# An attention, MoE and MoE kernel: thresholds and reciprocal sums placed behind later scores' bias, the bias as a one-operand multiplication, zero products in the first unit

## The chip, the cores and the metric

The kernel runs on one core of one Trainium2 chip. The metric is the device time of one execution in microseconds (us). An execution before the change takes 652.03 us in the median of three runs (651.8 to 654.82). The engines are TensorE (PE in the profile, with its weight loads as PEld), VectorE (DVE), ScalarE (ACT), GpSimd (POOL) and SyncE (SP), each with its own queue that runs in order.

## The reference

Three layers in a row. The first is an attention over 2 batches of 8 heads, 768 positions and 64 channels, in which a query sees a key only if the signs of six random projections agree:

```python
q_bits = (np.einsum('bhsd,dk->bhsk', q, proj) > 0).astype(np.int64)
k_bits = (np.einsum('bhsd,dk->bhsk', k, proj) > 0).astype(np.int64)
mask = q_bucket[:, :, :, None] == k_bucket[:, :, None, :]
scores = scale * np.matmul(q, k.transpose(0, 1, 3, 2))
scores = np.where(mask, scores, -1000000000.0)
scores = scores - np.max(scores, axis=-1, keepdims=True)
attn = np.exp(scores)
attn = attn / (np.sum(attn, axis=-1, keepdims=True) + 1e-09)
return np.matmul(attn, v).astype(np.float32)
```

Its result, as 1536 rows of 512, goes through a mixture of 8 experts with a fixed capacity (`x @ w_gate`, greedy assignment, two matrices per expert), and then through a second mixture with a skip gate and the best expert per row. The change touches the attention alone.

## The kernel before

Attention is cut into 16 units: a pair of heads and half of the queries (384). A unit has six score tiles of 128 queries by 768 keys, three per head. The mask is computed inside the score product: beside the 64 channels the key and query tiles carry 12 rows that hold thresholded projections, so that a pair with different signs gets a score that is lower by a large power of two. A head's keys are kept as K1 (a rounded copy) and K2 (the rest, and in rows 64 to 76 the thresholds); Q1 and Q2 are the same for queries.

For each tile, `score(u, i)` issues two products with Q1 and K1 (L197) and two with Q2 and K2 (L199) into one of two S buffers, and on the DVE a reduction over 768 keys (L201), the gate g (L202) and the bias b (L203). `expo` runs the exponential on ACT (L210), which reads S, b and g and frees the S buffer. Transposes (L219), their copies on ACT (L222) and the value products (L233) follow some tiles later. At tile 5 of the value products the sums get their reciprocal (L239, L240), which `fin` needs one unit later for the scaling of the rows it transposes back (L276 to L278).

While a unit runs, the next ones are prepared: `loadq` and `loadk` issue the DMAs on SP, `splitq` and `splitk` make Q1, Q2, K1 and K2 (a copy on DVE or, in unit 0, ACT; a subtraction on POOL, L139 and L152), and `project` multiplies queries and keys with the signs on PE (L168) into a small PSUM tile named aux, of which there is one copy. The thresholds (L174 for Q, L182 for K) read it on the DVE. `project` is a generator that stops once: the first two thresholds are issued at once, the others at the next odd tile (`left`). The tile of `fin` and the product tile of the routing counts (`count0`, L597) are taken from the same single buffer, tag aux.

Nothing is scheduled by a planner in this stage: the loop over units u and tiles i at the end of `attention` writes each engine's queue in the order of the calls. The tables `splits`, `projs` and `setup` say what is called at (u, i); `kplan` says which heads' keys are split in a unit: one head in units 0 to 4 and 9, two in units 5 to 8, none later. The second one of a unit is split and projected at tile 5. `awake` (L40) issues products of zeros whose result nobody reads; before the change there are 20 of them at the program's start.

## Time and profile before

| | |
|---|---|
| median of the runs | 652.03 us |
| the profiled execution | 652.32 us |
| its span, first to last instruction | 650.5 us |
| mean granted TensorE clock | 0.965 |
| PE busy | 597.1 us, 92% of the span |
| DVE busy | 494.0 us, 76% |
| ACT busy | 399.9 us, 61% |
| POOL busy | 162.9 us, 25% |
| reductions L201, 96 | 91.6 us, 18.7 idle before them |
| exponentials L210, 96 and their sums' reads | 95.1 us, 39.5 idle before them, 34.6 of it for the bias |

Attention fills the span's first 277 us or so, the two mixtures the rest. Shares of busy time are averages over these stages. A product counts as busy from its issue to its modelled end, and products overlap. The granted clock is given as a share of 2.4 GHz, and has two levels here, 1.0 and 0.5 (1.2 GHz). In a timeline row the bracket at its end gives how long the engine had been idle before it and who ended that.

### The profile page before, as it was taken

How to read it: one execution, taken by the hardware profiler on the slowest of the kernel's cores; microseconds unless marked ns; L12 is line 12 of the kernel's file. 1: busy time of each engine (PE TensorE's matmuls, PEld its weight loads, DVE VectorE, ACT ScalarE, POOL GpSimd, SP SyncE). 2: the span in 40 equal slices, each digit the busy share in tenths (PEclk: the TensorE clock that was granted, in tenths of full speed). 3: DMA queues.
4: the chain of work that ended last, by engine and by line, in shares of the span. 5: the costliest groups of instructions: out<-in, count | busy, mean ns of one | idle time of the engine just before them, and what ended most of it. 6: DMA issues, size and time to landing. Idle time of an engine off the chain costs nothing.

```text
span 650.5 us, 11417 instructions
## 1 busy us (share of the span) xinstructions
PE 597.1 (92%) x3781; PEld 434.6 (67%) x3781; DVE 494.0 (76%) x1542; ACT 399.9 (61%) x909; POOL 162.9 (25%) x212
## 2 busy tenths in 40 slices
PE   7889989999999999866878899999999999999994
PEld 3666666666666667745647487686786778777873
DVE  6888889999888786574958776877633467999991
ACT  4767767777677777412425654554554556887881
POOL 2245234334121120241013131221502322311110
PEclk8789999999999999957989999999999999999998
DMA  6114223312301010054367837458665379999800
GB/s 222 59 61 112 98 73 116 104 51 74 91 21 38 1 49 3 2 193 143 130 200 264 281 75 260 168 175 270 214 226 170 112 287 351 387 384 318 312 10 26
DMA packets 53240, 99.69 MB, mean 153 GB/s; under 512 B 6422, under 2 KB 12950, under 8 KB 53169
## 3 DMA queue, kind: packets, MB, share of 16 engines
q1 hardware_dynamic: 42016, 76.21, 34.9%
q10 hardware_dynamic: 7072, 13.63, 5.8%
q0 software_dynamic: 4080, 8.99, 4.2%
q8 instruction: 34, 0.56, 0.4%
q14 instruction: 38, 0.30, 0.2%
HBM read 88.72 MB, written 12.46 MB: 156 GB/s over the span
## 4 chain that ended last, share of the span: by engine, by line
PE 30%; DVE 10%; issue 6%; DMA 4%; ACT 2%; POOL 1%; POOLq 0%; DVEq 0%; ACTq 0%
PE ph L1173 10%; PE y L1198 6%; DVE wlo L1360 5%; PE y L1204 4%; DMA out<-o,ixi 3%; PE pr L1242 1%; DMA xg<-xd,idsb 1%; PE py L1422 1%; PE py L1421 1%; PE py L1420 1%; PE pxt L1152 1%; PE ph L1420 1%; ACT whi L1359 1%; PE ph L1421 1%; PE ph L1422 1%
## 5 line engine op out<-in xcount | busy, mean ns | idle before, releaser
L1360 DVE TENSOR_TENSOR wlo<-w,whi 128x512 fp32r<-128x512 f32 x192 | 123.7, 686 | 24.9 <-ACT whi L1359 20.9
L210 ACT ACTIVATE P<-S,b,g 128x768 f32<-128x768 f32 x96 | 95.1, 991 | 39.5 <-DVE b L203 34.6
L1359 ACT ACTIVATE whi<-w 128x512 fp32r<-128x512 f32 x192 | 109.4, 622 | 0.4 <-issue 0.4
L1173 PE MATMUL ph<-xT,w 128*128 128x192 f32 x512 | 103.3, 346 | 4.6 <-PEq L1526 4.6
L201 DVE TENSOR_REDUCE nm<-S 128x1 f32<-128x768 f32 x96 | 91.6, 954 | 18.7 <-PE S L199 17.1
L1173 PEld LDWEIGHTS ph<-xT,w 128*128 128x128 f32 x512 | 84.3, 195 | 13.9 <-issue 8.4
L222 ACT ACTIVATE PT<-pT 128x512 f32<-128x512 f32 x135 | 75.8, 593 | 25.6 <-PE pT L219 24.5
L219 PE MATMUL pT<-idf,P 128*128 128x128 f32 x576 | 81.3, 277 | 0.5 <-ACT PT L225 0.3
L219 PEld LDWEIGHTS pT<-idf,P 128*128 128x128 f32 x576 | 68.1, 143 | 5.7 <-ACT mrow L576 0.8
L197 PE MATMUL S<-K,Q 128*128 128x512 f32 x192 | 60.1, 395 | 12.8 <-ACT P L210 12.2
L233 PE MATMUL av<-PT,vd 128*64 128x384 f32 x360 | 67.8, 498 | 0.0
L197 PEld LDWEIGHTS S<-K,Q 128*128 128x128 f32 x192 | 30.1, 197 | 44.3 <-issue 21.4
L152 POOL TENSOR_TENSOR Q<-qd,Q 64x384 fp32r<-64x384 f32 x30 | 36.2, 1208 | 79.4 <-PE av L233 28.5
L1178 ACT ACTIVATE h<-ph 128x128 f32<-128x128 f32 x64 | 17.7, 276 | 60.5 <-PE ph L1173 29.5
L199 PE MATMUL S<-K,Q 76*128 76x512 f32 x192 | 51.0, 348 | 1.8 <-DVE Q L174 1.8
L233 PEld LDWEIGHTS av<-PT,vd 128*64 128x64 f32 x360 | 22.0, 136 | 23.8 <-issue 23.8
L199 PEld LDWEIGHTS S<-K,Q 76*128 76x128 f32 x192 | 30.6, 195 | 6.4 <-issue 2.1
L139 POOL TENSOR_TENSOR K<-kd,K 64x768 fp32r<-64x768 f32 x15 | 27.2, 1814 | 27.3 <-DVE K L130 18.8
L1204 PE MATMUL y<-w,h 128*64 128x512 f32 x128 | 32.3, 610 | 0.0
L1321 POOL DMA_INDIRECT tb<-rec,ii x16 | 16.0, 999 | 64.7 <-DVE cnt L1318 48.4
L1422 PE MATMUL py<-whi,hl 128*128 128x512 f32 x72 | 29.3, 406 | 1.4 <-DVE hl L1431 1.4
L1462 POOL DMA_INDIRECT out<-o,ixi x9 | 10.5, 1169 | 79.1 <-DVE o L1454 47.1
(374 smaller groups left out, 1125.1 us busy)
## 6 DMA issues: line engine op xcount, KB each, us to landing
w<-w SPq DMA_DIRECT2D x28, 1024.0 KB
w<-u SPq DMA_DIRECT2D x26, 1024.0 KB
kd<-kT SPq DMA_DIRECT2D x16, 384.0 KB
qd<-qT SPq DMA_DIRECT2D x32, 192.0 KB
w<-u ACTq DMA_DIRECT2D x6, 1024.0 KB
w<-w ACTq DMA_DIRECT2D x4, 1024.0 KB
xd<-X SPq DMA_DIRECT2D x4, 780.0 KB
vd<-v SPq DMA_DIRECT2D x16, 192.0 KB
```

What stands on the lines that cost most here:

```text
L197: nc.tensor.matmul(S[:, n0:n1], d["Q1", a][:, ts], kd["K1"][:, n0:n1], start=True, stop=False)
L199: nc.tensor.matmul(S[:, n0:n1], d["Q2", a][:, ts], kd["K2"][:, n0:n1], start=False, stop=True)
L201: nc.vector.tensor_reduce(d["nm"][:, c], S, op=ALU.max, axis=AX.X, negate=True)
L210: nc.scalar.activation(P, S, AF.Exp, bias=d["b"][:, c], scale=d["g"][:, c], accum_out=d["s"][:, c])
L219: nc.tensor.transpose(p[:, a, b, :], d["P"][2 * ip + b][:, (2 * cp + a) * 128:(2 * cp + a + 1) * 128], self.idf)
L222: nc.scalar.activation(dst, p.rearrange("p a b q -> p a (b q)"), AF.Copy)
L233: nc.tensor.matmul(d["av"][64 * a:64 * a + 64, :], VH[b * 8 + 2 * p + a][:, c, :], d["PT"][:, c, a * 384:(a + 1) * 384], start=(c == 0), s ...
L1173: nc.tensor.matmul(ph, w1[f // 4][:, d, f % 4 * 128:f % 4 * 128 + 128], xT[:, d, :], start=(d == 0), stop=(d == 3))
L1204: nc.tensor.matmul(y2[64 * h:64 * h + 64, :], h2[:, 4 * h + f, :], res["w2"][h][:, f, :], start=(f == 0), stop=(f == 3))
L1359: nc.scalar.activation(hi[:, c, :], w[:, c, :], AF.Copy)
L1360: nc.vector.tensor_tensor(lo[:, c, :], w[:, c, :], hi[:, c, :].bitcast(F32), op=ALU.subtract)
L1422: nc.tensor.matmul(out, a[1][:, i, :], hi[:, i % 4, :], start=False, stop=stop)
```

## The change

Four edits, all in `attention`.

`project` no longer issues thresholds. It issues the products and returns the generators, and the loop puts each threshold either at once or into a table `due`, under the number of a later score tile; `score` takes what is due for its tile and issues it behind the tile's bias. Of the four thresholds of a unit's projection at tile 1, the first stays there, the second goes behind the bias of tile 2, the K pair behind that of tile 4. Of a projection at tile 5 (units 5 to 8), one K threshold stays, the second goes behind the bias of the next unit's tile 0. At the program's start the second Q threshold goes behind the bias of tile 0, and the K pair of head 1 behind that of tile 1. Sums and reciprocal, now in `sums`, go behind the bias of tile 4, one tile later than before.

The bias b is computed by `tensor_scalar` with the gate as a per-partition scalar, where it was a `tensor_tensor` of two tiles.

In unit 0, 20 products of zeros stand between the first tile's two kinds of score products, and 5 behind each of tiles 1, 2 and 3. They write the transposes' PSUM tile.

In unit 0, the splits are issued behind the exponential of their tile, and that of head 2 moves from tile 1 to tile 2. `keys` makes K1 and K2 for whichever comes first, the split or a threshold.

```diff
             def project(fs, tag="aux"):
                 gs = [f(x, y, p[32 * i:32 * i + 12], i) for i, (f, x, y) in enumerate(fs)]
                 for g in gs:
                     next(g)
-                for i, g in enumerate(gs):
-                    next(g)
-                    if i == 1:
-                        yield
+                return gs
...
+                g0 = u * 6 + i
...
+                if g0 == 0:
+                    busy(20)
                 for n0, n1 in ((0, 512), (512, 768)):
                     nc.tensor.matmul(S[:, n0:n1], d["Q2", a][:, ts], kd["K2"][:, n0:n1], start=False, stop=True)
...
-                nc.vector.tensor_tensor(d["b"][:, c], d["g"][:, c], d["nm"][:, c], op=ALU.mult)
+                nc.vector.tensor_scalar(d["b"][:, c], d["nm"][:, c], d["g"][:, c], None, op0=ALU.mult)
+                for f in due.pop(g0, []):
+                    f()
+                if 0 < g0 < 4:
+                    busy(5)
+
+            def busy(k):
+                self.awake(ps.tile([128, 2, 2, 128], F32, name="pT", bufs=2).rearrange("p a b q -> p (a b q)")[:, 0:256], k)
...
-                    r = d["r"] = sm.tile([128, 6], F32, name="r")
-                    nc.vector.tensor_scalar(r, d["s"], 1e-9, None, op0=ALU.add)
-                    nc.vector.reciprocal(r, r)
+            def sums(u):
+                r = UD[u]["r"] = sm.tile([128, 6], F32, name="r")
+                nc.vector.tensor_scalar(r, UD[u]["s"], 1e-9, None, op0=ALU.add)
+                nc.vector.reciprocal(r, r)
...
-            for _ in project([(projk, 0, 0), (projk, 0, 1), (projq, 0, 0), (projq, 0, 1)]):
-                pass
+            due = {}
+            x = project([(projk, 0, 0), (projk, 0, 1), (projq, 0, 0), (projq, 0, 1)])
+            for f in x[:3]:
+                next(f)
+            due[0] = [lambda f=x[3]: next(f)]
...
+            for u in range(2, NU):
+                due.setdefault(u * 6 + 4, []).append(lambda u=u: sums(u - 2))
...
-                    for f, *x in splits.get((u, i), []):
-                        f(*x, ceng=nc.scalar if u == 0 else nc.vector)
+                    for f, *x in splits.get((u, i), []) if u else []:
+                        f(*x)
...
                     expo(u, i)
+                    for f, *x in [] if u else splits.get((u, i), []):
+                        f(*x, ceng=nc.scalar)
...
                         if (u, i) in projs:
-                            left = project(projs[u, i])
-                            next(left, None)
+                            fs = project(projs[u, i])
+
+                            at = (g + 1, g + 1, g + 1, g + 1) if u == 0 and i == 0 else (g, g + 1, g + 3, g + 3)
+                            for f, x in zip(fs, at):
+                                if x == g:
+                                    next(f)
+                                else:
+                                    due.setdefault(x, []).append(lambda f=f: next(f))
```

On the DVE at the program's start, the first two score tiles (nm, g and b are reduction, gate and bias; K2 and Q2 with a number are the threshold rows of head 0, of the first two query tiles, and of head 1). Before:

```order
L182 TENSOR_SCALAR K2_144<-aux_163,thr_77 12x384 x2
L174 TENSOR_SCALAR Q2_150<-aux_163,thr_77 12x384
L174 TENSOR_SCALAR Q2_159<-aux_163,thr_77 12x384
L201 TENSOR_REDUCE nm_184<-S_188 128x1
L202 TENSOR_SCALAR g_185<-nm_184 128x1
L203 TENSOR_TENSOR b_186<-g_185,nm_184 128x1
L182 TENSOR_SCALAR K2_173<-aux_198,thr_77 12x384 x2
L201 TENSOR_REDUCE nm_184<-S_203 128x1
```

The same place now:

```order
L185 TENSOR_SCALAR K2_144<-aux_163,thr_77 12x384 x2
L177 TENSOR_SCALAR Q2_150<-aux_163,thr_77 12x384
L207 TENSOR_REDUCE nm_183<-S_187 128x1
L208 TENSOR_SCALAR g_184<-nm_183 128x1
L209 TENSOR_SCALAR b_185<-nm_183,g_184 128x1
L177 TENSOR_SCALAR Q2_159<-aux_163,thr_77 12x384
L207 TENSOR_REDUCE nm_183<-S_222 128x1
L208 TENSOR_SCALAR g_184<-nm_183 128x1
L209 TENSOR_SCALAR b_185<-nm_183,g_184 128x1
L185 TENSOR_SCALAR K2_172<-aux_219,thr_77 12x384 x2
```

The second Q threshold, the last reader of the first aux tile, has moved behind the first bias, and the K pair of head 1, the last reader of the second aux tile, behind the second bias.

On PE at the same place, from the end of the first score tile to the second's end; aux_219 is the projection of head 1's keys, in the buffer that aux_163 had. Before:

```order
L199 MATMUL S_188<-K2_144,Q2_150 128x256
L168 MATMUL aux_198<-kd_141,prs_135 12x384 x2
L197 MATMUL S_203<-K1_143,Q1_149 128x512
L197 MATMUL S_203<-K1_143,Q1_149 128x256
L199 MATMUL S_203<-K2_144,Q2_150 128x512
L199 MATMUL S_203<-K2_144,Q2_150 128x256
L168 MATMUL aux_230<-qd_180,prs_135 12x384
```

The same place now, with the last of the 20 zero products ahead and the first of five behind:

```order
L40 MATMUL pT_190<-zero_71 128x256
L205 MATMUL S_187<-K2_144,Q2_150 128x512
L205 MATMUL S_187<-K2_144,Q2_150 128x256
L171 MATMUL aux_219<-kd_141,prs_135 12x384 x2
L201 MATMUL S_222<-K1_143,Q1_149 128x512
L201 MATMUL S_222<-K1_143,Q1_149 128x256
L205 MATMUL S_222<-K2_144,Q2_150 128x512
L205 MATMUL S_222<-K2_144,Q2_150 128x256
L40 LDWEIGHTS zero_71
L40 MATMUL pT_232<-zero_71 128x256
```

PE's projection still stands ahead of the second score tile; only zero products are new in its queue.

On the DVE from tile 5 of unit 5 to tile 0 of unit 6 (K1 and K2 with a number belong to the second head that unit 5 splits; lt and X are the scaling of `fin`'s result). Before:

```order
L203 TENSOR_TENSOR b_1079<-g_1078,nm_1077 128x1
L130 CAST K1_1245<-kd_946 128x768
L182 TENSOR_SCALAR K2_1246<-aux_1262,thr_77 12x384 x2
L201 TENSOR_REDUCE nm_1267<-S_1271 128x1
L202 TENSOR_SCALAR g_1268<-nm_1267 128x1
L203 TENSOR_TENSOR b_1269<-g_1268,nm_1267 128x1
L257 TENSOR_TENSOR lt_1297<-fin_1293,r_1209 128x48
L278 TENSOR_TENSOR X_94<-fin_1293,r_1209 128x3x128
```

The same place now:

```order
L209 TENSOR_SCALAR b_1118<-nm_1116,g_1117 128x1
L130 CAST K1_1284<-kd_985 128x768
L185 TENSOR_SCALAR K2_1285<-aux_1301,thr_77 12x384
L207 TENSOR_REDUCE nm_1305<-S_1309 128x1
L208 TENSOR_SCALAR g_1306<-nm_1305 128x1
L209 TENSOR_SCALAR b_1307<-nm_1305,g_1306 128x1
L185 TENSOR_SCALAR K2_1285<-aux_1301,thr_77 12x384
L272 TENSOR_TENSOR lt_1336<-fin_1332,r_1256 128x48
L293 TENSOR_TENSOR X_94<-fin_1332,r_1256 128x3x128
```

One of the two thresholds has moved from ahead of unit 6's first reduction to behind its first bias.

## Rows read from the trace of the kernel before

**Rows 1.** Windows: us, engines' busy us (instructions), granted clock, DMA share, GB/s.

```profile
38.14:277.00 238.86, 229.69 (x1647) 157.20 (x1646) 198.46 (x511) 171.80 (x341) 68.45 (x101) 1.00 0.19 60
...
95.20:110.80 15.60, 15.51 (x104) 10.15 (x103) 14.72 (x35) 11.37 (x22) 6.52 (x7) 1.00 0.31 102
```

**Rows 2.** Timeline of PE at the starts of five units: start, us, instruction, idle before.

```profile
70.34 0.59 PE L197 MATMUL S<-K,Q 128*128 128x512 f32 x2 [0.91 <-ACT P L210]
...
86.69 0.59 PE L197 MATMUL S<-K,Q 128*128 128x512 f32 x2 [1.72 <-ACT P L210]
...
166.18 0.60 PE L197 MATMUL S<-K,Q 128*128 128x512 f32 x2 [1.61 <-ACT P L210]
...
197.40 0.60 PE L197 MATMUL S<-K,Q 128*128 128x512 f32 x2 [1.08 <-ACT P L210]
...
243.54 0.60 PE L197 MATMUL S<-K,Q 128*128 128x512 f32 x2 [0.92 <-ACT P L210]
```

**Rows 3.** Groups of DVE instructions, 8 to 262 us: busy us, mean ns, idle before.

```profile
L201 DVE TENSOR_REDUCE nm<-S 128x1 f32<-128x768 f32 x96 | 91.6, 954 | 18.7 <-PE S L199 17.1
L182 DVE TENSOR_SCALAR K<-aux,thr 12x384 fp32r<-12x384 f32 x32 | 19.7, 615 | 0.6
...
L203 DVE TENSOR_TENSOR b<-g,nm 128x1 f32<-128x1 f32 x96 | 17.1, 178 | 3.3
L202 DVE TENSOR_SCALAR g<-nm 128x1 f32<-128x1 f32 x96 | 14.8, 154 | 3.3
L239 DVE TENSOR_SCALAR r<-s 128x6 f32<-128x6 f32 x15 | 11.3, 750 | 0.0
```

**Rows 4.** Timeline of the first unit, all engines.

```profile
9.41 1.27 DVE L174 TENSOR_SCALAR Q<-aux,thr 12x384 fp32r<-12x384 f32 x2
...
10.17 0.59 PE L199 MATMUL S<-K,Q 76*128 76x512 f32 x2 [1.78 <-DVE Q L174]
...
10.74 1.43 PE L168 MATMUL aux<-kd,prs 64*12 64x384 f32 x4
...
14.96 1.81 POOL L139 TENSOR_TENSOR K<-kd,K 64x768 fp32r<-64x768 f32 x1
14.97 1.82 DVE L203 TENSOR_TENSOR b<-g,nm 128x1 f32<-128x1 f32 x1
...
19.52 0.99 ACT L210 ACTIVATE P<-S,b,g 128x768 f32<-128x768 f32 x1 [1.56 <-DVE b L203]
```

**Rows 5.** Timeline of PE, zero products: all 20, the last six, the last five.

```profile
1.09 3.75 PE L40 MATMUL S<-zero 128*128 128x256 bf16 x20 [1.09 <-DVE zero L52]
...
4.02 0.82 PE L40 MATMUL S<-zero 128*128 128x256 bf16 x6
...
4.13 0.71 PE L40 MATMUL S<-zero 128*128 128x256 bf16 x5
```

**Rows 6.** Windows: a stretch of the first unit.

```profile
10.83:14.20 3.37, 3.37 (x12) 1.19 (x14) 2.88 (x6) 1.96 (x5) 0.33 (x1) 0.50 0.62 236
```

**Rows 7.** Timeline of DVE and PE at the start of unit 6.

```profile
102.59 1.23 DVE L182 TENSOR_SCALAR K<-aux,thr 12x384 fp32r<-12x384 f32 x2
...
102.93 1.04 PE L219 MATMUL pT<-idf,P 128*128 128x128 f32 x8
...
103.88 1.00 PE L276 MATMUL fin<-R,OT 128*128 128x144 f32 x6
```

**Rows 8.** Timeline: sums and subtraction in unit 5, sums in 9, count product in 10.

```profile
96.94 1.01 POOL L152 TENSOR_TENSOR Q<-qd,Q 64x384 fp32r<-64x384 f32 x1 [1.70 <-issue]
96.99 0.98 DVE L239 TENSOR_SCALAR r<-s 128x6 f32<-128x6 f32 x1
...
97.34 0.52 PE L199 MATMUL S<-K,Q 76*128 76x512 f32 x2
...
161.84 0.15 DVE L239 TENSOR_SCALAR r<-s 128x6 f32<-128x6 f32 x1
...
174.42 0.38 PE L597 MATMUL pcq<-oh,gn 128*128 128x8 bf16 x9
```

More of the change, by code (lines that the diff above doesn't have):

```diff
@@ L130, in copy, with keys @@
                     eng.tensor_copy(out, a)
+            def keys(g):
+                d = KH[g]
+                if "K1" not in d:
+                    d["K1"] = kp.tile([128, 768], F32R, name="K1")
+                    d["K2"] = kp.tile([76, 768], F32R, name="K2")
+                return d["K1"], d["K2"]
             def splitk(g, eng=nc.gpsimd, ceng=nc.vector, n=1):
                 d = KH[g]
-                K1 = d["K1"] = kp.tile([128, 768], F32R, name="K1")
-                K2 = d["K2"] = kp.tile([76, 768], F32R, name="K2")
+                K1, K2 = keys(g)
                 for j in range(n):
@@ L181, in projk @@
                 yield
-                nc.vector.tensor_scalar(d["K2"][64:76, sl], p, self.thr[:, 1:2], -BIG, op0=ALU.is_gt, op1=ALU.mult)
+                nc.vector.tensor_scalar(keys(g)[1][64:76, sl], p, self.thr[:, 1:2], -BIG, op0=ALU.is_gt, op1=ALU.mult)
                 yield
@@ L344, in attention @@
             nload = 1
-            projs, splits = {}, {}
+            projs = {}
+            splits = {(0, 2): [(splitk, order[0])]}
             for u in range(NU):
@@ L351, in attention @@
                 for x, g in enumerate(kplan.get(u, [])):
-                    splits.setdefault((u, 1 + 4 * x), []).append((splitk, g))
+                    if u:
+                        splits.setdefault((u, 1 + 4 * x), []).append((splitk, g))
                     for j in range(2):
@@ L357, in attention @@
             projs[0, 0] = [(projk, 1, 0), (projk, 1, 1)]
-            left = None
+            for u in range(2, NU):
+                due.setdefault(u * 6 + 4, []).append(lambda u=u: sums(u - 2))
             for u in range(NU):
@@ L394, in attention @@
                     if i % 2 or u == 0:
-                        if left:
-                            next(left, None)
-                            left = None
                         if (u, i) in projs:
-                            left = project(projs[u, i])
-                            next(left, None)
+                            fs = project(projs[u, i])
[5 more added lines that the diff above has]
+                                    due.setdefault(x, []).append(lambda f=f: next(f))
                     if i == 0 and u >= 3:
@@ L415, in attention @@
                 av(L - 1, c)
+            sums(L - 1)
             last_av(0)
```

## The prediction

> **What bounds the kernel now.** I read the windows view by stage first, then the waits of TensorE (PE) and its timeline. In the windows the reader is to see that from 38 to 277 us the attention stage runs at the full granted clock with PE busy 229.7 of 238.9 us, and that one unit, 95.2 to 110.8, has 15.51 busy of 15.60, with VectorE (DVE) at 14.72 right behind [rows 1]. So in that stage a microsecond counts only if PE waits for it. The timeline shows where PE does wait: the first score product of a unit stands for an exponential 0.91 before 70.34, 1.72 before 86.69, 1.61 before 166.18, 1.08 before 197.40 and 0.92 before 243.54 [rows 2]. Behind attention the same instructions follow in the same order; I let all of it shift one to one.
>
> **The change part by part.** The profiled execution took 652.32 us (650.5 span, 1.82 around it); the median of the runs is 652.03, so 0.29 is taken off at the end.
>
> *Units 2 to 15, the gain.* Before tile 4 of a unit the DVE has sums, reciprocal and the pair of K thresholds ahead of the reduction: 0.75 in the mean for the sums, 0.615 for a threshold; reduction, gate and bias take 0.954, 0.154 and 0.16, with the gaps about 1.3 [rows 3]. Moved behind the bias, sums and pair let tile 4's exponential start up to 2 us sooner, more than any wait of rows 2. The waits of 0.91, 1.72 and 1.08 go whole. Of 1.61 I count 1.0: tile 5's reduction now stands behind sums, K pair and a counting step of that unit, so the second tile of the next unit is late next. Of 0.92 I count 0.75 for a like reason. That is 5.46; other units start with about 0.1 of idle time (15.60 less 15.51), four of them hold 0.4. Gain 5.9 (4.5 to 6.7).
>
> *Units 5 to 8, a new wait.* These split a second key head. Its two thresholds stood together behind tile 5; now the second stands behind the bias of the next unit's tile 0. The buffer aux has one copy, and `fin` of the next unit is the next to write it, on PE. In unit 6 the pair began at 102.59, so it ended at 103.8, and `fin` began at 103.88, right behind eight transposes that began at 102.93 [rows 7]. Now it is 102.59 + 0.615 + 1.3 + 0.615 and two gaps, 105.2, and `fin` at 105.3. PE stands 1.4 us longer; queued behind `fin` are score tile 1, its transposes and the value products, and with 0.1 us of slack in the unit all of it is lost. Four units, 5.6 us. Ends: 1.1 each if the reduction starts the moment its score is done (4.4), 2.2 each if the DVE arrives 0.83 late (8.8).
>
> *Units 10 and 12.* The count product, at 174.42 in unit 10 [rows 8], takes aux behind the second Q threshold, which now follows the bias of tile 2: one threshold more, less about 0.1 for the earlier reduction. 0.5 each, 1.0 (0 to 1.3).
>
> *The opening.* Tile 0's second products waited 1.78 us for a threshold of the pair begun at 9.41, and ran from 10.17 for 0.59; the next projection began at 10.74, right behind the second Q threshold (9.41 + 1.27) [rows 4]. That threshold is now behind tile 0's bias. The 20 zero products step at 0.11 us at full clock (the group of six starts at 4.02, its last five at 4.13) [rows 5]: 2.2 us, into a hole of 1.78 that PE can enter about 0.2 early. So tile 0 is 0.2 late: 10.17 + 0.2 + 0.59 + 1.3 + 0.615 = 12.9, and only then starts the projection (10.74 before), with score tile 1 behind it in PE's queue. The projection took 1.43 at the low clock [rows 4], so about 0.75 at the full one; a score tile takes about 1.0, 1.7 at the low one. Score 1 ends at 14.7 to 15.3, its bias at 16.0 to 16.6. Before, that bias took 1.82, from 14.97 to 16.79, beside a GpSimd subtraction of 1.81 from 14.96 [rows 4]. The one-operand form ends this stall, and the late score eats what it saves. Next, the K pair (1.23) follows that bias, unit 1's projection waits for it until 17.3 to 17.9, score 2 follows, 1.75 to 3.1 for both, then 1.3: its exponential starts at 20.4 to 22.3 instead of 19.52 [rows 4]. Unit 1 gives back about 1.0, since its K pair too moves out of the way. Left: 0 to 1.8 late. The five zero products behind tiles 1 to 3 run while PE has nothing else. The granted clock was 0.50, 1.2 GHz, from 10.83 to 14.20, right after the wait of 1.78 [rows 6]; the new waits, about 2.0 and then 1.2 to 2.5, look like that one, so I stay near the upper end: +1.3. Ends: -0.4 (all of it covered), +3.4 (zero products at the first twenty's mean, 3.75 for 20 [rows 5], 1.6 more).
>
> In the Trainium skill, "TensorE: Matmul & The Clock Gate", Part 1, throttled is the default and activity releases it. By that rule the zero products hold the clock up and the opening costs 0; by the row of a wait followed by the low level it costs 1.3. The first is rival B.
>
> *Bias form and sums.* All 96 biases sum to 17.1 us, mean 178 ns; the gate, already one-operand on one column, has 154 [rows 3]. 96 x 24 ns is 2.3, of which 1.66 is the one long case, counted above; the rest lies beside PE work: zero (gain 0.6, or the same as a loss, since PE has that slack in the units). Sums took 0.98 at 96.99 while a GpSimd subtraction ran from 96.94 for 1.01, and 0.15 at 161.84 [rows 8]. Their new place is behind tile 4's bias; its score ends at 97.86 [rows 8], and 1.3 later that subtraction is over: 0.15, and hidden.
>
> The Trainium skill, "SBUF — State Buffer", Who interferes with whom, says that DVE and GpSimd contend for a shared port pair, and counts `tensor_scalar` among what can take it. The 0.98 agrees. By that rule the sums can be caught in the new place too, by the row they are not: rival D.
>
> *Sum.* -5.9 + 5.6 + 1.0 + 1.3 = +2.0: 654.3 for the profile, 654.0 against the median.
>
> **Rivals.**
> A. The waits for aux are covered and the change only gives: 1.3 - 5.9 = -4.6, 647.4. For it: thresholds leave the path of tile 4 in every unit. Against: aux has one copy, and PE had 0.09 us idle in that unit. 0.17.
> B. The clock stays at 2.4 GHz through unit 0 and the opening costs nothing: +0.7, 652.7. For it: the zero products fill the hole of 1.78. Against: two new holes behind it. 0.15.
> C. Slower: PE's clock is already low when the 20 zero products begin near 8.2. They take 3.75 or more, tile 0 and all behind it slip 1.6, the opening costs 3.4: +4.1, 656.1. It decides from where they end later than 10.03, when the threshold that they cover is done, by more than the 0.2 above. For it: the first twenty took 3.75. Against: the five at 4.13 were fast. 0.10.
> D. Sums are caught by GpSimd in their new place: 0.83 more (0.98 less 0.15) ahead of K pair and reduction 5, on the path to `fin` in four units: +3.3 on the forecast, 657.3. Against: GpSimd was done by then in the unit shown. 0.08.
> That the change does not do what it says I rule out: the order shows each move.
>
> **How the numbers follow.** Forecast 0.50, A 0.17, B 0.15, C 0.10, D 0.08. The forecast's own range is 651.5 to 656.5; with the rivals, 649.5 to 658.0 leaves about 2 in 10 out, mostly A. A measurement tells 0.5% (3.3 us) from no change. Faster (below 648.8): most of A, 0.16. Slower (above 655.3): a quarter of the forecast, most of C and D, 0.30. Within: 0.54.
>
> **What would show it.** Right: PE waits of 1.2 to 1.6 us before `fin` at the start of units 6 to 9, put down to the K threshold; no wait of a first score product above 0.7 in units 3 to 15; projections in the first unit that start near 13 and near 17.5; no bias longer than 0.3. Wrong: `fin` following its transposes at once, a granted clock of 1.0 from 4 to 38 us, or sums of 0.9 behind tile 4. If units 6 to 9 are not about 1.4 us longer than now, the forecast has failed at its largest term.

## The result, and the profile after

The changed kernel took 663.18 us in the median of four executions (659.59 to 663.6), the kernel before 651.91 in four beside it (651.68 to 654.82): 1.0149 times the time, 95% interval 1.0115 to 1.0182. Measured again in six executions (fifth experiment) it took 662.87, 1.014 [1.0101, 1.018]. The forecast was 654.0 with a range up to 658.0; the time lies outside it, on the slow side. The profiled execution after took 663.6 (span 661.7), 11.3 above the one before.

The windows of the profile after (us, busy us and instructions of PE, PEld, DVE, ACT, POOL, granted clock, DMA share, GB/s) show the same work over attention as [rows 1], now in 244.49 us, and the second stretch of [rows 1], one unit's length around the start of unit 6, in 17.10 us where it took 15.60. The third and fourth lines are stretches at half clock, one in the middle of attention, which had none before, and one in the first unit.

```profile
38.14:282.63 244.49, 232.11 (x1643) 158.19 (x1641) 196.08 (x511) 170.88 (x340) 68.94 (x101) 0.99 0.19 59
93.20:110.30 17.10, 15.42 (x103) 10.13 (x102) 14.38 (x35) 11.26 (x23) 6.46 (x6) 1.00 0.29 93
120.95:124.35 3.40, 3.40 (x16) 2.88 (x16) 1.61 (x3) 0.21 (x3) 0.47 (x2) 0.50 0.44 159
18.56:21.95 3.39, 3.39 (x15) 2.30 (x14) 2.83 (x7) 1.42 (x3) 0.00 (x0) 0.50 0.22 58
```

PE's timeline after (start, us, instruction, idle before it) at unit starts answers to [rows 2]: 0.91 and 1.72 are gone, 1.61 has become 0.46, 1.08 has become 0.32 and 0.92 has become 0.41. The row at 42.48, the start of unit 2, is a new wait that the prediction does not have.

```profile
42.48 0.61 PE L201 MATMUL S<-K,Q 128*128 128x512 f32 x2 [0.64 <-ACT P L223]
...
69.55 0.62 PE L201 MATMUL S<-K,Q 128*128 128x512 f32 x2
...
84.15 0.62 PE L201 MATMUL S<-K,Q 128*128 128x512 f32 x2
...
173.47 0.62 PE L201 MATMUL S<-K,Q 128*128 128x512 f32 x2 [0.46 <-ACT P L223]
...
199.43 0.62 PE L201 MATMUL S<-K,Q 128*128 128x512 f32 x2 [0.32 <-ACT P L223]
...
248.79 0.59 PE L201 MATMUL S<-K,Q 128*128 128x512 f32 x2 [0.41 <-ACT P L223]
```

What was gained there is lost at the next place. The timeline of DVE and PE at the start of unit 6 answers to [rows 7]: first K threshold, reduction, bias, second K threshold stand in a row on DVE, and `fin` waits for the last of them. The same wait stands ahead of `fin` in units 7 to 9.

```profile
100.59 0.61 DVE L185 TENSOR_SCALAR K<-aux,thr 12x384 fp32r<-12x384 f32 x1
...
101.23 0.96 DVE L207 TENSOR_REDUCE nm<-S 128x1 f32<-128x768 f32 x1
...
102.41 0.21 DVE L209 TENSOR_SCALAR b<-nm,g 128x1 f32<-128x1 f32 x1
...
102.66 0.61 DVE L185 TENSOR_SCALAR K<-aux,thr 12x384 fp32r<-12x384 f32 x1
...
103.33 1.00 PE L291 MATMUL fin<-R,OT 128*128 128x144 f32 x6 [1.68 <-DVE K L185]
...
120.60 0.78 PE L291 MATMUL fin<-R,OT 128*128 128x144 f32 x3 [1.68 <-DVE K L185]
...
139.43 0.76 PE L291 MATMUL fin<-R,OT 128*128 128x144 f32 x4 [1.67 <-DVE K L185]
...
156.70 0.51 PE L291 MATMUL fin<-R,OT 128*128 128x144 f32 x2 [1.67 <-DVE K L185]
```

Count products in units 10 and 12, which before started without a wait [rows 8]:

```profile
180.11 0.37 PE L625 MATMUL pcq<-oh,gn 128*128 128x8 bf16 x9 [0.56 <-DVE Q L177]
...
211.34 0.59 PE L625 MATMUL pcq<-oh,gn 128*128 128x8 bf16 x18 [0.55 <-DVE Q L177]
```

The DVE groups of attention (busy us, mean ns, idle before) answer to [rows 3]. The one-operand bias takes 214 ns, not less than the two-operand one but more; the sums have fallen from 750 to 180.

```profile
L207 DVE TENSOR_REDUCE nm<-S 128x1 f32<-128x768 f32 x96 | 91.7, 955 | 24.0 <-PE S L205 22.6
L209 DVE TENSOR_SCALAR b<-nm,g 128x1 f32<-128x1 f32 x96 | 20.6, 214 | 3.4
...
L208 DVE TENSOR_SCALAR g<-nm 128x1 f32<-128x1 f32 x96 | 14.7, 153 | 3.3
...
L254 DVE TENSOR_SCALAR r<-s 128x6 f32<-128x6 f32 x15 | 2.7, 180 | 0.0
```

The first unit's timeline answers to [rows 4]: the zero products fill the hole of 1.78, no bias is caught, and both following projections wait on the aux bank, 2.14 and 2.19 us.

```profile
7.80 2.36 PE L40 MATMUL pT<-zero 128*128 128x256 bf16 x20
...
9.92 0.59 PE L205 MATMUL S<-K,Q 76*128 76x512 f32 x2
...
11.73 0.21 DVE L209 TENSOR_SCALAR b<-nm,g 128x1 f32<-128x1 f32 x1
...
12.65 0.82 PE L171 MATMUL aux<-kd,prs 64*12 64x384 f32 x4 [2.14 <-DVE Q L177]
...
17.11 0.50 PE L171 MATMUL aux<-qd,prs 64*12 64x384 f32 x2 [2.19 <-DVE K L185]
```

Matching the two profiles instruction by instruction, the changed kernel is 0.1 us late at the first exponential of unit 2, 5.6 at the last one of attention, and 11.3 at PE's last instruction. So in this pair of profiles as much was lost behind attention, where nothing was changed, as in it. The largest piece there, 2.8 us, stands behind a wait that both kernels have: PE waits 2.83 us for VectorE's `yr` ahead of the second expert's last transposes. The rows show that wait and the six microseconds behind it, first before, then after; granted clock 1.00 in the one, 0.50 in the other.

```profile
370.09 0.46 PE L1242 MATMUL pr<-idf,yr 64*128 64x64 f32 x4 [2.83 <-DVE yr L1237]
```

```profile
370.10:376.10 6.00, 6.00 (x65) 5.06 (x65) 3.20 (x14) 2.93 (x11) 0.00 (x0) 1.00 0.63 240
```

```profile
377.64 0.69 PE L1270 MATMUL pr<-idf,yr 64*128 64x64 f32 x4 [2.83 <-DVE yr L1265]
```

```profile
377.64:383.64 6.00, 6.00 (x29) 4.43 (x30) 2.12 (x6) 2.02 (x7) 0.00 (x0) 0.50 0.69 262
```

### The profile page after: what moved, and what is told of

It reads as the page before. It is cut to its first block, busy times and chain, and to the rows that moved or that the text cites. A ratio compares the mean times of both kernels' runs of the same rounds, so it can differ in the third digit from the quotient of the medians.

```text
span 661.7 us, 11488 instructions
## 1 busy us (share of the span) xinstructions
PE 604.5 (91%) x3816; PEld 439.6 (66%) x3816; DVE 489.8 (74%) x1542; ACT 399.6 (60%) x909; POOL 163.8 (25%) x212
## 4 chain that ended last, share of the span: by engine, by line
PE 30%; DVE 9%; issue 6%; DMA 5%; ACT 1%; POOL 1%; POOLq 0%; SPq 0%; ACTq 0%
PE ph L1201 10%; PE y L1226 5%; PE y L1232 4%; DVE wlo L1388 4%; DMA out<-o,ixi 3%; PE pr L1270 1%; DMA xg<-xd,idsb 1%; PE py L1450 1%; PE ph L1448 1%; PE py L1449 1%; PE py L1448 1%; PE ph L1449 1%; PE ph L1450 1%; PE pxt L1180 1%; ACT whi L1387 1%
## 5 line engine op out<-in xcount | busy, mean ns | idle before, releaser
L1201 PE MATMUL ph<-xT,w 128*128 128x192 f32 x512 | 105.9, 352 | 4.1 <-PEq L1554 4.1
L1201 PEld LDWEIGHTS ph<-xT,w 128*128 128x128 f32 x512 | 86.4, 199 | 14.6 <-issue 9.9
L232 PEld LDWEIGHTS pT<-idf,P 128*128 128x128 f32 x576 | 66.7, 141 | 6.4 <-ACT PT L235 1.0
L855 POOL CAST idf<-idsb 128x2 f32<-128x2 int32 x7 | 2.4, 338 | 111.9 <-DVE idsb L851 111.9
```

The lines of the kernel that those rows point to most:

```text
L232: nc.tensor.transpose(p[:, a, b, :], d["P"][2 * ip + b][:, (2 * cp + a) * 128:(2 * cp + a + 1) * 128], self.idf)
L1201: nc.tensor.matmul(ph, w1[f // 4][:, d, f % 4 * 128:f % 4 * 128 + 128], xT[:, d, :], start=(d == 0), stop=(d == 3))
```

## The experiments

Theory at the start: inside attention, the waits ahead of `fin` are the loss; behind it, PE has the same waits as before, but the granted clock falls behind them in one execution and not in another. Rivals: the lost time belongs to DVE's work in its new order; the loss behind attention belongs to the change. All ratios are against the kernel before in executions beside it (its medians: 653.29, 653.16, 652.32 and 653.29 in the four groups, 17 to 30 executions each). "By the ratios" means a difference of two such ratios, in us of the kernel before; it is known to some 2 to 3 us.

**1. The two-threshold projections back in one place.** The condition also puts the Q pairs of units 10 to 14 back to tile 1, which the expectation does not say.

```diff
                             at = (g + 1, g + 1, g + 1, g + 1) if u == 0 and i == 0 else (g, g + 1, g + 3, g + 3)
+                            if u and len(fs) == 2:
+                                at = (g, g)
```

> The changed kernel with one thing put back: where a unit projects a second head's K (units 5 to 8, tile 5), both of its thresholds stand at tile 5, none behind the next unit's first bias. Theory (the four waits of fin on the aux bank are the largest loss inside attention): the four PE waits of 1.67 us ahead of fin (at 101.65, 118.92, 137.76 and 155.03 us of the profile after) fall below 0.1 each, and the half-clock stretch at 120.95 to 124.36 that follows the second one goes; attention ends 5 to 8 us earlier than in the changed kernel, that is within 2.5 us of the kernel before. Rival (VectorE's time behind the waits is the limit, so the two thresholds at tile 5 cost the next unit's first score product as much): fin's waits go, but waits of 1 us or more stand ahead of L199's first product in units 6 to 9, and attention ends less than 3 us earlier. Behind attention: if the loss there depends on where the same waits fall against the granted clock, it changes by several us in either direction; if it belongs to the change itself, it stays near 5.7 us. Total 655 to 658 us by the first, about 657.5 by the last, over 660 by the rival.

Measured: 652.43 us, 0.9986 [0.9963, 1.0008], under every time named. The waits ahead of `fin` fall to 0.23, not below 0.1, the half-clock stretch beside them goes, and no first score product of units 6 to 9 waits instead. The first theory holds as to the waits; attention ends 8.9 us earlier than in the changed kernel, more than the 5 to 8 expected. The gain over the changed kernel is 10.0 us by the ratios, for waits of 4 x 1.68 and 2 x 0.55, 7.8 us; the 2 us between the two are within the noise.

```profile
101.13 1.23 DVE L185 TENSOR_SCALAR K<-aux,thr 12x384 fp32r<-12x384 f32 x2
...
102.42 1.00 PE L291 MATMUL fin<-R,OT 128*128 128x144 f32 x6 [0.23 <-DVE K L185]
```

**2. PE's wait for `yr` filled, in the changed kernel.**

```diff
             pt = ps.tile([128, 4, w], F32, name="pr", tag="rows", bufs=2)
+            if p == 1 and hf:
+                n.awake(pt.rearrange("p d q -> p (d q)"), 26)
```

> The changed kernel with 26 zero products (256 columns each, into the bank that the pr transposes then overwrite) placed ahead of the transposes of the second expert's last rows, so that PE has work in its wait of 2.83 us for VectorE's yr (374.81 to 377.64 us after). Nothing else moves. Theory (this wait, standing elsewhere against the clock than before the change, is what let the granted clock fall to 0.50 at 376.95 to 383.78): the clock stays 1.00 there, the 6.8 us at half clock are spared, and the total falls by about 3.4 us, to 659.5 to 660.5. Rival (the clock falls there for another reason, or the work there is bound by VectorE or the transfers of weights): the total stays within 1 us of the changed kernel's 663, or grows by up to 1 us for the products.

Measured: 658.51, 1.0096 [1.0066, 1.0126], 655.22 to 663.14 in 12 executions. By the ratios that is 2.9 us below the changed kernel, not clear of the noise by itself, and a little under the theory's 659.5. The products end when `yr` is there, and the six microseconds behind them run at 1.00. The spread of 8 us is left, so this wait isn't all of it.

```profile
371.23 3.00 PE L40 MATMUL pr<-zero 128*128 128x256 bf16 x26
374.23 0.46 PE L1272 MATMUL pr<-idf,yr 64*128 64x64 f32 x4
```

```profile
374.23:380.23 6.00, 6.00 (x66) 5.06 (x65) 3.20 (x14) 2.93 (x11) 0.00 (x0) 1.00 0.68 253
```

**3 and 4. Pure delays in the kernel before**, 52 and 32 zero products ahead of one score tile.

```diff
                 ts = slice(t * 128, (t + 1) * 128)
+                if u == 12 and i == 2:
+                    self.awake(S[:, 0:256], 52)   # 32 in the fourth
```

> The kernel before with 52 zero products of 256 columns (about 0.107 us each at full clock, 5.6 us together) in front of one score tile in the middle of attention (unit 12, tile 2), where PE is busy without a wait. No threshold, sum or bias is moved. Theory (the 5.7 us that the changed kernel lost behind attention come from the same waits falling elsewhere against the granted clock, and any shift of 5.6 us does that): attention ends 5.6 us later and the time behind it grows too, by 3 to 6 us, with half-clock stretches that the kernel before does not have; total 660.5 to 664. Rival (the loss behind attention belongs to the moved work): a pure shift, total 657.5 +- 0.7.

> As the delay of 52, with 32 zero products (3.4 us). Theory (losses behind attention depend on how far the shift carries the waits against the granted clock): the extra behind attention differs from that of the delay of 52, and may be near zero; total 655.3 if it is, up to 661 if not. Rival (a pure shift): 655.3 +- 0.7, and 2.2 us below the delay of 52. A third view (the loss comes as soon as anything is later): as much extra as with 52.

Measured: 660.66, 1.0099 [1.0063, 1.0134], and 658.13, 1.0076 [1.0048, 1.0103]. Attention got 5.5 and 3.4 us longer, as built. As ratios, pure shifts would be 1.0085 and 1.0053: both lie inside the intervals, so the times do not decide. The profiles do show that a kernel whose thresholds were not touched can lose behind attention too: 4.5 us after the longer delay (of it 3.6 at the first expert, where PE waited 8.20 us for weights), 2.2 after the shorter one. In the shorter one's profile the clock is at half from 371.0 to 377.8 us, behind the wait for `yr`.

**5. The changed kernel again.**

> The changed kernel itself, unaltered, in more executions beside the kernel before, because executions of one kernel spread over 5 to 8 us here (the kernel before 649.4 to 656.2 in 25 executions, the kernel with the filled wait 655.2 to 663.1). Theory (about 2 to 5 of the 11 us by which the two profiles differ are where one execution's waits fell against the granted clock, the rest is attention's 5.6 us and what follows it): median 660 to 662.5, spread of 4 to 8 us, 1.011 to 1.014 times the kernel before. Rival (the loss behind attention belongs to the change and comes in every execution): median 663 +- 0.7 with a spread under 2 us.

Measured: 662.87, 1.014 [1.0101, 1.018], 659.03 to 664.89. The median is the rival's (663 +- 0.7), a little above the theory's 662.5; the spread of 5.9 is the theory's. So the times leave both open, and the profile of this execution decides against the rival's mechanism: against the profile before it is 9.8 us late at the last exponential of attention and 11.1 at the end. The same kernel lost 5.7 us behind attention in its first profile and 1.3 in this one. Behind the same wait for `yr`, where its clock was 0.50 the first time, it is 1.00:

```profile
380.41 0.46 PE L1270 MATMUL pr<-idf,yr 64*128 64x64 f32 x4 [2.84 <-DVE yr L1265]
```

```profile
380.41:386.41 6.00, 6.00 (x65) 5.06 (x65) 3.20 (x14) 2.93 (x11) 0.00 (x0) 1.00 0.76 280
```

This execution had two half-clock stretches in attention, at 106.3 and 160.9, which begin 0.4 and 1.6 us behind the start of a `fin` that had waited; the first had one, at 120.95, 0.4 behind; the profile of the second experiment has none. Matched against that last one, each costs 1.6 us.

**6. The bias alone**, in the kernel before.

```diff
-                nc.vector.tensor_tensor(d["b"][:, c], d["g"][:, c], d["nm"][:, c], op=ALU.mult)
+                nc.vector.tensor_scalar(d["b"][:, c], d["nm"][:, c], d["g"][:, c], None, op0=ALU.mult)
```

> The kernel before with one edit: the bias as one-operand multiplication (tensor_scalar) in place of tensor_tensor, all else as before. Theory (the bias gave nothing but in the first unit, where one bias waited 1.82 us): the first unit's bias of 1.82 us falls to 0.2, the median instruction stays near 0.2 us, and the total is within 0.7 us of the kernel before. Rival (the bias is what shortened units 2 to 15): the total is 3 us or more below the kernel before.

Measured: 657.07, 1.0062 [1.0036, 1.0087]. Neither expectation: it is slower by 4 us. The stall of 1.82 is gone, but all 96 biases take 213 to 216 ns, where the median before was 159. The first score products of rows 2 wait longer for it (1.72 became 1.88, 1.61 became 1.76), and behind each of these two the clock is now at 0.50, which it was in none of four profiles with the old bias in the old order.

```profile
L203 DVE TENSOR_SCALAR b<-nm,g 128x1 f32<-128x1 f32 x96 | 20.6, 214 | 3.4
...
L239 DVE TENSOR_SCALAR r<-s 128x6 f32<-128x6 f32 x14 | 12.0, 854 | 0.0
```

```profile
85.10 0.60 PE L197 MATMUL S<-K,Q 128*128 128x512 f32 x2 [1.88 <-ACT P L210]
```

```profile
86.95:90.05 3.10, 3.10 (x14) 2.90 (x14) 1.34 (x6) 1.75 (x4) 0.47 (x2) 0.50 0.00 0
168.57:171.95 3.38, 3.38 (x15) 3.19 (x14) 1.58 (x5) 2.18 (x5) 0.68 (x3) 0.50 0.00 0
```

**7. The opening of the kernel before**, on top of the first experiment.

```diff
-                if g0 == 0:
-                    busy(20)
...
-                if 0 < g0 < 4:
-                    busy(5)
...
-            for f in x[:3]:
+            for f in x:
                 next(f)
-            due[0] = [lambda f=x[3]: next(f)]
...
-                            at = (g + 1, g + 1, g + 1, g + 1) if u == 0 and i == 0 else (g, g + 1, g + 3, g + 3)
+                            at = (g, g, g + 1, g + 1) if u == 0 else (g, g + 1, g + 3, g + 3)
```

> The changed kernel with the two-threshold projections put back to one place (as in the first experiment: K in units 5 to 8 at tile 5, and Q in units 10 to 14 at tile 1) and with the opening of the kernel before: all four thresholds of the first projection at once, those of the second at once, no zero products in the first unit, the split of the third K at tile 1. Theory (the new opening costs 1.3 us where the clock does the same in both, as predicted; in the two profiles it looked free because the kernel before had more half-clock time in its opening): 1 to 2 us below the first experiment, 650.5 to 651.5. Rival (zero products pay for the waits on the aux bank by keeping the clock up): equal to the first experiment within 0.7 us, or slower.

Measured: 650.31, 0.9962 [0.9942, 0.9982], 2.1 us below the first experiment (1.6 by the ratios). The two intervals overlap, but the profiles agree that the opening did cost, though the first pair of them showed 0.1: at the first exponential of unit 2 all six with the new opening are later than all ten with the old one. (The profile of the seventh is the fastest of its 14 executions, 4.6 us under their median.)

**8. The seventh with the fill of the second.**

> The seventh experiment's kernel with the 26 zero products of the second one in PE's wait for yr of the second expert. Theory (the wait lets the granted clock fall in most executions, and the fill spares some 3 us on the mean): 647.5 to 649.5, 1 us or more under the lowest median of the others and 3 to 5 under the kernel before. Rival (the fill paid only because that wait stood badly in the changed kernel): within 1 us of the seventh experiment.

Measured: 646.63, 0.9901 [0.9869, 0.9933], and all six executions within 646.41 to 647.65. Faster than both kernels.

**9 and 10. The seventh and the eighth with the two-operand bias.**

> The seventh experiment's kernel with the bias of the kernel before (two operands, tensor_tensor): what is left of the change is the sums and the first K pair behind tile 4's bias and the second Q threshold behind tile 2's (units 1 to 9). Theory (the one-operand bias costs 55 ns on each of 96 tiles, 214 against 159, and through PE's waits and the clock beside them 4 us in the sixth experiment; the moves give the predicted 5.9): 1.5 to 4.5 us below the seventh experiment, 646 to 649, and 4.5 to 7 below the kernel before. Rival (behind the moves DVE has slack, so the bias's form costs nothing there): within 1 us of the seventh experiment's 650.3.

> The ninth experiment's kernel with the 26 zero products in PE's wait for yr of the second expert. Theory (bias form and fill add up): 643 to 645.5, below the eighth experiment's 646.6 by 1 to 3.5 us, and the fastest of all. Rival (bias form is covered once the moves are made): 646.6 +- 0.7.

Measured: 650.58, 0.9965 [0.9933, 0.9997], and 646.58, 0.9902 [0.9866, 0.9937]: as the seventh and the eighth, so the rival's numbers are right in both: behind the moved thresholds the bias's form costs nothing that the times can tell. Its reason, slack on DVE, is not shown, since two things changed against each other. In the new order the two-operand bias is itself held beside GpSimd (it ends only as a GpSimd subtraction does), in ten of 96 tiles in each of the two profiles (0.26 to 0.92 us, and once 1.79), so that its mean in the ninth is 194 ns, not far from 214. And `fin`, which waits 4 x 0.23 us with the one-operand bias and an unsplit pair, does not wait here: it starts as its transposes end. The ninth profile's bias group, one held bias, and `fin` of unit 6:

```profile
L207 DVE TENSOR_TENSOR b<-g,nm 128x1 f32<-128x1 f32 x96 | 18.6, 194 | 3.3
```

```profile
98.85 1.24 DVE L185 TENSOR_SCALAR K<-aux,thr 12x384 fp32r<-12x384 f32 x2
...
99.12 1.04 PE L228 MATMUL pT<-idf,P 128*128 128x128 f32 x8
...
100.14 1.00 PE L287 MATMUL fin<-R,OT 128*128 128x144 f32 x6
...
105.23 1.82 POOL L145 TENSOR_TENSOR K<-kd,K 64x768 fp32r<-64x768 f32 x1
...
106.60 0.47 DVE L207 TENSOR_TENSOR b<-g,nm 128x1 f32<-128x1 f32 x1
```

The ninth's 12 executions fall into six of 648.0 to 649.3 and six of 651.9 to 655.5; in its profile the clock falls behind the wait for `yr`, just as in the changed kernel, with none of the `fin` waits in it.

```profile
366.65 0.58 PE L1264 MATMUL pr<-idf,yr 64*128 64x64 f32 x3 [2.83 <-DVE yr L1259]
```

```profile
366.65:372.65 6.00, 6.00 (x29) 4.43 (x30) 2.11 (x6) 2.02 (x7) 0.00 (x0) 0.50 0.65 249
```

**11. Only the K pairs back**, the Q pairs left split.

```diff
+                            if u and i == 5:
+                                at = (g, g)
```

> The changed kernel with only the second head's K pair of units 5 to 8 put back to tile 5; the Q pairs of units 10 to 14 stay split over two biases, unlike in the first experiment. Theory (the four waits ahead of fin, 1.67 us each, and the half-clock time beside them are what the first experiment took away; the count product's two waits of 0.55 are the rest): 653 to 654.5, that is 8.5 to 10 us below the changed kernel's 662.9, and 0.5 to 2 us above the first experiment's 652.4. Rival (the Q pairs carry a good part of it): 656 or more.

Measured: 655.27, 1.0033 [1.0001, 1.0065]. Between the two expectations: 7.0 us below the changed kernel by the ratios. In its profile attention behind unit 2's start is 5.8 us shorter than in the second experiment's, which is 4 x 1.68 less the 4 x 0.235 that `fin` still waits. Against the first experiment's profile it is 2.1 us longer there: that is what splitting the Q pairs of units 10 to 14 costs. Two waits of 0.56 at the count product are half of it; first score products wait 0.33 at unit 12 and 0.42 at unit 15, which they do not in the first experiment.

**12. The fill in the kernel before**, with the diff of the second.

> The kernel before with the same 26 zero products in PE's wait for yr of the second expert, nothing else. In its profile the clock stayed at 1.00 behind that wait. Theory (that was one execution's luck; in most executions the clock falls there in the kernel before as well): 2 to 3.5 us below the kernel before, 649.5 to 651. Rival (the kernel before has its clock there in every execution, the fall belongs to the changed kernel): within 0.7 us of it.

Measured: 650.05, 0.9962 [0.9938, 0.9987], all 12 executions within 649.08 to 651.48, where the kernel before spreads over 648.8 to 657.6 beside it. So the clock falls at that wait in part of the executions of the kernel before as well; this is concluded from the times, and the profiles of the fourth and sixth experiments, which have the old order of thresholds, show it. The mean granted clock of each execution, which is on record with its time, says the same of the whole spread: of 95 executions of the kernel before, the fastest 23 have 0.967 in the mean (650.4 us), the slowest 23 have 0.959 (655.3 us).

**13. The four waits ahead of `fin` filled too**, on top of the second.

```diff
                     if i == 0 and u >= 3:
+                        if 6 <= u <= 9:
+                            UD[u]["early"] = ps.tile([128, 768], F32, name="S", bufs=2)
+                            self.awake(UD[u]["early"][:, 0:256], 15)
                         fin(u - 3)
```

> The second experiment's kernel with 15 more zero products (about 1.6 us) in each of the four PE waits ahead of fin at the start of units 6 to 9, into the score bank that the unit's tile 1 then overwrites. The waits' own 4 x 1.68 us stay, since the K threshold is no earlier. Three profiles of kernels with these waits show none, one and two half-clock stretches beside them. Theory (the waits cost what they last and, in part of the executions, half-clock time beside them; this is why taking them away gave more than they last): the spread of 7.9 us of the second experiment falls under 3.5 us and the median falls by 1.5 to 3 us, to 655.5 to 657. Rival (the four waits cost what they last, the spread comes from elsewhere): median 658 to 659.5, spread over 6 us.

Measured: 659.7, 1.011 [1.0078, 1.0143], 657.29 to 662.85. Nearest to the rival (658 to 659.5, spread over 6): no gain, and the spread of 5.6 stays. Half-clock time beside these waits is seen in single executions, but that it makes the median is not shown.

**14. The bias alone, with the fill**: the sixth and the twelfth together.

> The kernel before with the one-operand bias and the 26 zero products in PE's wait for yr, so that only attention and the opening can differ from the twelfth experiment (650.05, spread 2.4 us). The sixth experiment was 4 us slower than the kernel before, the ninth as fast as the seventh. Theory (in the kernel before's order the bias stands on the path of the units with first-score waits of 1.7 us: 55 ns a tile make these waits longer and the clock falls beside them): 652.5 to 655, with a spread of 3 us or more. Rival (the sixth experiment's 4 us came from the wait for yr, which the fill takes away): 649.5 to 651.5, spread under 3 us.

Measured: 655.26, 1.0025 [1.0003, 1.0047]: 4.1 us above the twelfth by the ratios, spread 5.7, with the same two half-clock stretches, at 86.9 and 168.9. 0.3 above the theory's range and far from the rival's: the bias's loss is in attention.

The shifts of the profiles against that of the kernel before, in us, at four places (first exponential of unit 2, last one of attention, second expert's first `pr`, PE's last instruction), as worked out from matched instructions:

| kernel | unit 2 | end of attention | second expert | end |
|---|---|---|---|---|
| after / again (5) | 0.1 / 2.7 | 5.6 / 9.8 | 7.6 / 10.3 | 11.3 / 11.1 |
| 1, pairs back | 0.6 | -3.3 | -3.2 | -0.6 |
| 2, after + fill | 1.0 | 5.0 | 4.1 | 3.9 |
| 3 / 4, delays | -1.6 / -1.7 | 3.9 / 1.8 | 8.7 / 1.2 | 8.4 / 3.9 |
| 6, bias alone | -2.0 | 3.1 | 4.0 | 6.7 |
| 7 / 8 | -2.4 / -2.0 | -6.3 / -6.0 | -6.6 / -4.6 | -6.5 / -4.6 |
| 9 / 10 | -1.4 / -0.3 | -5.5 / -4.5 | -3.4 / -4.7 | 1.2 / -4.8 |
| 11, K pairs back | 2.4 | 0.6 | 2.9 | 6.2 |
| 12, before + fill | -1.2 | -1.2 | -1.9 | -2.1 |
| 13 / 14 | 0.9 / -1.7 | 4.8 / 3.3 | 6.9 / 4.2 | 7.0 / 4.1 |

## Why the prediction was wrong, step by step

**Units 2 to 15, -5.9.** Right in direction, a third too large. From unit 2 to the end of attention the moves with no pair split gave 4.1 in the ninth and the tenth profile (3.9 to 4.0 in the first, seventh and eighth). By PE's first score products in the ninth profile the waits of 0.91, 1.72, 1.08 and 0.92 were gained whole. Of 1.61, where I counted 1.0, nothing was: 0.39 is left there and 0.74 stands ahead of the next tile (unit 9 starts at 149.10 before and 145.42 in the ninth, unit 11 at 181.03 and 177.51). From unit 5 to unit 9, where I counted a small gain, 0.5 was lost. The sums fell to 160 ns in the median from 978, as the row at 161.84 [rows 8] suggested, and rival D fell with that.

**Units 5 to 8, +5.6.** Right, mechanism and size. The DVE chain was right: I had `fin` 2.7 us behind the start of its K pair, and it is 103.33 less 100.59, 2.74. The four waits are 1.67 to 1.68, not 1.4, but 0.23 to 0.24 of each stand there with an unsplit pair too wherever the bias has one operand (first, seventh, eighth and eleventh experiment), and not where it has two (ninth and tenth). Splitting the K pairs cost the rest: 5.8 us inside attention (eleventh against second experiment). Rival A, that the waits for aux are covered, is out.

**Units 10 and 12, +1.0.** The two waits are right: 0.56 and 0.55. The price is not: splitting the Q pairs cost 2.1 us (eleventh against first experiment), since first score products at units 12 and 15 keep waits by it that I counted as gained.

So attention behind unit 2 should have come out at -5.9 + 5.6 + 1.0 = +0.7. Without half-clock stretches it is +4.0 (second and thirteenth profile), and the runs, each against the next, make it up: -3.9 for the moves (with the 4 x 0.23 ahead of `fin` in it), 5.8 for the K pairs, 2.1 for the Q pairs. Here is the step that failed first: "Gain 5.9 (4.5 to 6.7)" is 3.9 to 4.1, outside its own range, and "1.0 (0 to 1.3)" is 2.1, outside its own range as well; they missed to the same side, by 3.1 together. The price of the K pairs, 5.6, was right.

**The opening, +1.3.** 1.6 us by the ratios of the first and seventh experiments, 2.7 as the mean of the profiles (first exponential of unit 2: six with the new opening, ten with the old), inside the bounds. The waits were those predicted (about 2.0 and 1.2 to 2.5; measured 2.14 and 2.19). Rival C did not come about: the 20 zero products took 2.36 us, not 3.75. Rival B's mechanism was there in part of the executions and did not win: in four of the six profiles with the new opening the clock stays at 1.00 until after 18 us and the opening has 3.4 us at half clock, where the old one has 10.2 to 17.1; in the other two (fifth and eleventh experiment) it falls near 14 us, 0.7 to 0.8 us behind the end of the first wait of 2.14, and they have 10.2. Unit 2's first exponential is 0.1 to 1.0 late in the four and 2.4 to 2.7 in the two, and all are later than any profile of the old opening.

**The bias, 0.** Not refuted for this kernel, but for the wrong reason. I took the gate's 154 ns for a one-operand instruction's price; it is 214. Alone, in the old order, the new bias costs 4 us, twice (sixth against before, fourteenth against twelfth), where both profiles show 5.0 between unit 2 and the end of attention, 3 of them in the two half-clock stretches. Behind the moved thresholds it costs nothing that the times can tell (seventh against ninth, eighth against tenth), and that is luck: there it adds 4 x 0.23 us ahead of `fin` and spares ten held biases. I had put the whole of attention's slack under it without asking which units have none.

**"Behind attention [...] I let all of it shift one to one."** This failed in the two profiles compared, by 5.7 us, and they mislead: what is lost there differs from execution to execution (5.7 and 1.3 us in two of the changed kernel itself), and the profile before, against which I summed, was one that lost little. Untouched thresholds with a delay lost 4.5 and 2.2 there, the ninth kernel 6.6, the seventh nothing. Filling the wait for `yr` takes about as much off the kernel before (2.5 us) as off the changed one (2.9), and 2.4 to 4.1 off the sixth, seventh and ninth, so that wait tells the profiles apart and not the kernels.

**The sum.** Of the 9.1 us that the ratio of 1.014 means, 4.0 are attention without half-clock stretches and 1.6 to 2.7 the opening; the forecast had 0.7 and 1.3. Some 2.4 to 3.5 us stay open. The likeliest place is a term that the prediction put at nothing without a reason: a fall of the clock behind the new waits in attention, though its own [rows 6] show one right behind a wait of 1.78 us. Three profiles have the four waits of `fin` unfilled, and three such stretches between them (one, two and none), 1.6 us each, so 1.6 in the mean. Against it, filling these waits in the thirteenth experiment gained nothing, though six executions do not rule out a part. Nor has the changed kernel more half-clock time in all: its mean granted clock is 0.963 in the median of ten executions, as in 95 of the kernel before. It could have as much of it at places where it costs more; no run here separates that.

## What to carry to other kernels

When a step is moved behind another engine's wait, write down which bank or buffer it then frees later and who takes that next: here one threshold of each of four pairs, which cost nothing where it stood, held a single bank for some 1.45 us more each time, 5.8 us together, more than all that the moves gave. Where one engine's wait can drop its own clock, the wait's price is not its length, and one profile does not give it: compare several executions, and try filling the wait, which here alone (0.9962) was worth as much as the moves alone (0.9965).

## What the runs showed of the hardware that was not expected

A VectorE `tensor_scalar` on one column takes 211 to 217 ns when its operand is a column in memory (960 of them in ten profiles), 152 to 157 with two constants, and the two-operand `tensor_tensor` 159 in the median. The first of these was never held beside GpSimd, though 7 to 16 of each 96 ran while a GpSimd `tensor_tensor` did. The two-operand one was held in one or two of 96 in the old order, the longest for 1.82 us, and in ten of 96 in the new order (ninth and tenth profile).

Executions of the unchanged kernel before spread over 6.4 to 8.8 us in four groups (648.8 to 657.6 in the widest), and 26 zero products in one wait of 2.83 us bring that to 2.4. The Trainium skill, "TensorE: Matmul & The Clock Gate", Part 1, calls the time that a kernel's start spends at the low clock variable from run to run. The runs agree (half clock in the old opening: 10.2 to 17.1 us in ten profiles), and they show the same of waits in the middle of a kernel: behind one and the same unfilled wait of 2.83 us the clock was 1.00 in four profiles (before, third, fifth, seventh) and 0.50 in six (after, first, fourth, sixth, ninth, eleventh). The changed kernel itself stands in both lists.
